# A threshold attention with two gated layers behind it: one triple of cast weights kept on chip, whole-bank ranks, and three edits behind the attention

## The chip, the cores and the metric

One core of one Trainium2 chip runs the whole program. The metric is device time in microseconds (us) of one execution, the median over runs.

## The reference, cut to what matters

```python
def _attn_ref(q, k, v, tau):                       # 4 batches, 8 heads, 576 rows, head size 64
    scores = np.matmul(q, k.transpose(0, 1, 3, 2)) / np.sqrt(q.shape[-1])
    thresh = np.max(scores, axis=-1, keepdims=True) - tau
    scores = np.where(scores >= thresh, scores, -1000000000.0)
    attn = softmax(scores)
    return np.matmul(attn, v)

x = attn_out as 2304 tokens x 512
gate = 1 / (1 + np.exp(-(x @ w_gate)))             # 512 x 1536
x = (gate * (x @ w_val)) @ w_out                   # 512 x 1536, 1536 x 512
h = ((x @ w1) * (x @ w2)) @ w3                     # 512 x 1024, 512 x 1024, 1024 x 1024
out = h @ w_out2                                   # 1024 x 512
```

The weights arrive in 64 bits, q, k and v in 32 bits.

## The kernel before, in words

Matmuls of fp32 accuracy are made from halves: `split` (line 818) rounds a block to fp32r on ScalarE (`hi`, line 822) and subtracts on GpSimd or VectorE (`lo`, line 823), and `three` (line 825) adds the three products hi x lo, lo x hi and hi x hi in one PSUM bank. All matmuls have line 439 in the profile, so they are told apart by the names of their tiles.

**The attention.** Sixteen pairs of heads with nine slices each, 144 slices. A slice is scores on TensorE (`ps_s`, from `xq`, `yq`, `xk`, `yk`, or for the ninth slice of a pair the block-diagonal `qbd`), a maximum on VectorE (line 687), two ScalarE passes (lines 695 and 696), a split into two fp16 halves on ScalarE and GpSimd (lines 703 and 707), a DMA transpose (line 711, tile `pt`) and the product with v (`u` or `ps_s`, fp16; a PV run below). Two buffers, `ps_s0` and `ps_s1`, serve all slices in turn. At the end of a pair TensorE transposes the result (`ps_x`, `ps_s` from `ident`), and ScalarE copies it to `XR` (lines 774 and 776).

**Filler beside it.** `merge_gen` first multiplies w3 by w_out2 once for all tokens (`ps<-wo,t`), and stores the merged blocks to DRAM (`sc_m`). Then `l1_gen` (line 937) computes the gated layer in four passes over tokens: three of 512 tokens, and a last one of 768 tokens that runs behind the attention. In a pass, twelve blocks F follow each other; a block is `h_unit` (24 matmuls in two banks `ps_h`), and after each third block `o_stage` (line 1077) adds three blocks' products with w_out to the tokens: four `o_unit`s with 9 matmuls each into a bank `ps_o`, and a VectorE addition into `XR`. A stage is held in `pend` and emitted after the next block's `h_unit`. So the last stage of the third pass is emitted after the first block of the last pass.

**Cast weights.** In the first pass the 64-bit weights are loaded in blocks (`XR<-in_moe_w...`, 512 KB) and cast on VectorE, ScalarE and GpSimd (`cast64`, line 796) into a triple `w` of a gate, a value and an output block (768 KB, two buffers). `usplit` (line 981) splits a block and stores the finished triple to DRAM (`sc_w`, line 989); in the later passes `uload32` (line 975) loads the triple back (line 979). `tick` (line 996) spreads these steps over the matmuls. All these DMAs are issued on SP's queue, in order, with the transposes and the loads of q, k and v.

**The order.** Up to the end of the attention the order of every engine is made by the class `Plan`: `order` (line 229) lists the instructions by a forecast of times, taking among the ready ones that of the lowest rank; `backward` (line 322) turns that into new ranks, by the latest start; `pin` (line 365) does this ROUNDS times (line 38) and pins the order with the earliest forecast end of TensorE. `kind` (line 185) names a matmul's form: H for 16 bits, T for plain fp32, R for fp32r of 64 rows, and W for other fp32r. Behind the attention the order is made by the framework's scheduler, which takes ready instructions by their place in the program.

**Behind the attention.** The last pass runs beside the preparation of w1 and w2 (`w12_gen`). Then three groups of 768 tokens follow. A group is a seven-product scheme for x @ w1 and x @ w2 (`pair`, `ps_ab`) on operands made by `x2split` (line 1331: two subtractions on VectorE, two on GpSimd, and seven splits), their product split into `abh` and `abl`, and the output stage (`ps_y`): for each of eight merged blocks `part` does 18 matmuls. `wm_load` (line 1461) loads a merged block and splits it into `wm`, which has two buffers; the split of block i + 2 is emitted behind part i. The last two parts are taken together, tile by tile, each tile going out as it is done.

Of the kernel before, what the change touches and what calls it, by code (L numbers as in the profile page):

```python
# [8 lines left out]
F32 = mybir.dt.float32  # L9
F32R = mybir.dt.float32r  # L10
F16 = mybir.dt.float16
BF16 = mybir.dt.bfloat16
I32 = mybir.dt.int32
# [8 lines left out]
class Plan:  # L22
# [12 lines left out]
    STAY = 0  # L35
    NEAR = ("HH", "RH", "TH", "HT", "RT", "TT")
    TURN = {"HW": 86, "RW": 199, "WR": 90, "HR": 90, "TR": 90, "RH": 100, "RT": 145, "TW": 5, "HT": 34}
    ROUNDS = 6

    def __init__(self, insts, cut, over, beads=()):  # L40
        self.later = [i for i in insts[cut:] if i.opcode in self.OPS]
# [280 lines left out]
    def backward(self):  # L322
        N, E = len(self.x), ("PE", "DVE", "ACT", "POOL", "SP")
        pred = [self.hard[n] | self.soft[n] for n in range(N)]
        out = [0] * N
        for n in range(N):
            for q in pred[n]:
                out[q] += 1
        lat = [d - s for s, d in zip(self.start, self.done)]
        held = [  # L330
            c[0] if e in ("PE", "SP") else max(60, c[0] - self.OVER[e])
            for c, e in zip(self.cost, self.e)
        ]
        ready, begin = [0.0] * N, [0.0] * N
        avail = {e: [n for n in range(N) if not out[n] and self.e[n] == e] for e in E}
        free = dict.fromkeys(E, 0.0)
        for _ in range(N):
            best = None
            for e in E:
                if not avail[e]:  # L340
                    continue
                n = min(avail[e], key=lambda n: (
                    max(ready[n] + lat[n] - held[n] - free[e] - 1, 0), -self.done[n]
                ))
                s = max(free[e], ready[n] + lat[n] - held[n])
                if best is None or s < best[0]:
                    best = s, e, n
            s, e, n = best
            avail[e].remove(n)
            begin[n] = free[e] = s + held[n]  # L350
            for q in pred[n]:
                out[q] -= 1
                if q not in self.hard[n]:
                    r = begin[n] - lat[q]
                elif self.e[q] == self.e[n] != "SP":
                    r = begin[n] - (lat[q] - 5 if e == "PE" else 0)
                else:
                    r = begin[n] + self.LAG[self.e[q]] + self.LEAD[e]
                ready[q] = max(ready[q], r)
                if not out[q]:  # L360
                    avail[self.e[q]].append(q)
        for i, n in enumerate(sorted(range(N), key=lambda n: -begin[n])):
            self.rank[n] = i

    def pin(self, tc):
        best = None
        for i in range(self.ROUNDS):
            seq = self.order()
            end = max(t for t, e in zip(self.done, self.e) if e == "PE")
            if best is None or end < best[0]:  # L370
                best = end, seq, self.start
            if i + 1 < self.ROUNDS:
                self.backward()
# [25 lines left out]
def kernel(  # L399
# [22 lines left out]
    nc = tc.nc  # L422
    P = 128
    B, H, S, D = q.shape
    NPAIR = H // 2
    NT, DM = out.shape
# [3 lines left out]
    NF = DFF // P  # L430
# [40 lines left out]
    ap_ = actx.enter_context(tc.tile_pool(name="attn", bufs=1, side="right"))  # L471
# [309 lines left out]
    UW = KC * P  # L781
    sc_w = [dram.tile([P, 3, UW], F32, name=f"sc_w{f}") for f in range(NF)]
# [51 lines left out]
    def flush(keep):  # L834
        while len(defer) > keep:
            defer.pop(0)()
# [84 lines left out]


    SG = 3
    lp = None
    lx = None
    lb = None
# [8 lines left out]
        lx = lx_ctx.enter_context(tc.tile_pool(name="lx", bufs=1))  # L935

    def l1_gen():
        w32, whl, gv, pend, raws = {}, {}, {}, [], {}
        NFT = B * NF
        units = []  # L940
        for F in range(NFT + 1):
# [2 lines left out]
        def unit(n):  # L944
            if n < len(units) and 0 <= units[n][1] < NFT:
                nm, F = units[n]
                return nm, F, F // NF, F % NF
            return None
# [8 lines left out]

        def packed(n):
            m = n // 3
            if m not in w32:  # L960
                w32[m] = lp.tile([P, 3, UW], I32, tag="w", name="w", bufs=2)
                w32.pop(m - 2, None)
            return w32[m]

        def ucast(n):
            u = unit(n)
# [7 lines left out]

        def uload32(n):
            m, j = divmod(n, 3)
            if unit(n) and m >= NF and j == (2 if m == NFT else 0):
                ks = slice(j, 2 if m == NF else 3)
                nc.sync.dma_start(packed(n)[:, ks].bitcast(F32), sc_w[m % NF][:, ks])

        def usplit(n):
            u = unit(n)
            if u:
                nm, F, b, f = u
                m, j = divmod(n, 3)
                x = w32[m][:, j]
                if b == 0 and j == (2 if m else 1):
                    ks = slice(2 if m == NF else 0, j + 1)
                    nc.sync.dma_start(sc_w[m % NF][:, ks], w32[m][:, ks].bitcast(F32))
                k = 4 if nm == "o" else 2  # L990
                hi = lp.tile([P, KC, P], F32R, tag=nm + "h", name=nm + "h", bufs=k)
                lo = lp.tile([P, KC, P], F32R, tag=nm + "l", name=nm + "l", bufs=k)
                split(hi, lo, x.bitcast(F32).rearrange("p (a b) -> p a b", a=KC))
                whl[nm, F] = (hi, lo)
# [7 lines left out]
        def xsplit(b):  # L1002
            o, k, w = passes[b]
            xh, xl = (lx.tile([P, KC, k * w], F32R, tag=z, name=z) for z in ("xh", "xl"))
            for j in range(k):
                js = slice(j * w, (j + 1) * w)
                for c in range(KC):
                    split(
                        xh[:, c, js], xl[:, c, js], XA[:, c, o + j * w:o + (j + 1) * w],
                        nc.vector if c % 2 else nc.gpsimd,  # L1010
                    )
            return xh, xl
# [41 lines left out]
        def o_unit(b, st_, c, j):  # L1054
            p0, k_, w = passes[b]
            ps = bank("ps_o")
            for i in range(SG):
                F = b * NF + st_ * SG + i
                hi, lo = whl["o", F]
# [33 lines left out]
        for F in range(NFT):  # L1093
            b, f = divmod(F, NF)
            if f == 0:
                while not ready(b):
                    yield None
                if b == B - 1:
                    lx_ctx.close()
                    open_lx()  # L1100
                xhl = xsplit(b)
            k, w = passes[b][1:]
            gv[F] = [
                tuple(
                    (lx if j else lb).tile([P, w], F32R, tag=g, name=g, bufs=4)
                    for g in ("gvh", "gvl")
                )
                for j in range(k)
            ]
            for j in range(k):  # L1110
                yield from h_unit(F, xhl, j)
            whl.pop(("g", F)), whl.pop(("v", F))
            if pend:
                yield from o_stage(*pend.pop())
            if f % SG == SG - 1:
                pend.append((b, f // SG))
                if F == NFT - 1:
                    flush(0)
                    yield from o_stage(*pend.pop())
                    flush(0)  # L1120
# [150 lines left out]
    NG = NT // GT  # L1271
# [86 lines left out]
    x2 = None  # L1358
    while x2 is None or l1 is not None:
        l1 = run(l1, 4200.0)  # L1360
        if next(wg_, "end") == "end" and x2 is None:
            wctx.close()
            xp = ctx.enter_context(tc.tile_pool(name="xp", bufs=1, side="right"))
            x2 = x2split(0)
# [3 lines left out]
    sp = ctx.enter_context(tc.tile_pool(name="sp", bufs=1))  # L1368
# [90 lines left out]
            at, c0, left = at + m, c0 + m, left - m  # L1459

    def wm_load(i):
        t = sp.tile([P, 2, DM], F32R, tag="wm", name="wm", bufs=2)
        x = sp.tile([P, DM], F32, tag="y", name="wms", bufs=4)
        nc.sync.dma_start(x, sc_m[i])
        split(t[:, 0], t[:, 1], x, nc.gpsimd if i % 2 else nc.vector)
        return t
# [3 lines left out]
    for g in range(NG):  # L1470
        abs_ = [
            tuple(sp.tile([P, GT], F32R, tag=f"ab{z}{f}", name=f"ab{z}{f}") for z in "hl")
            for f in range(NF2)
        ]
        for i in range(NPR):
            if i == NPR - 1:
                wms = [wm_load(0), wm_load(1)]
            pair(x2, i, abs_)
        if g + 1 < NG:
            x2 = x2split(g + 1)  # L1480
        pss = [bank("ps_y") for _ in range(GT // P)]
        def part(i, t):
            h, l = abs_[i]
            ts_ = slice(t * P, (t + 1) * P)
            three(
                pss[t], (h[:, ts_], l[:, ts_]), (wms[i][:, 0], wms[i][:, 1]), i == 0, i == NF2 - 1
            )

        for i in range(NF2 - 2):
            for t in range(GT // P):  # L1490
                part(i, t)
            wms.append(wm_load(i + 2))
        end = len(nc.cur_bb.bb.instructions)
        for t in range(GT // P):
            part(NF2 - 2, t)
            part(NF2 - 1, t)
            out_rows(g, t, pss[t])
# [36 lines left out]
```

## Time and profile before

| what | before |
|---|---|
| median of 3 runs | 1044.69 us (1042.97 to 1045.5) |
| the profiled execution | 1041.44 us |
| its span, first to last instruction | 1039.5 us |
| granted TensorE clock, mean | 0.995 of full |
| TensorE busy | 985.5 us, 95% |
| GpSimd, ScalarE, VectorE busy | 699.3, 652.9, 616.7 us |

The page gives busy times of one execution: PE is TensorE's matmuls, PEld its weight loads, DVE VectorE, ACT ScalarE, POOL GpSimd, SP the queue that issues the DMAs. Matmuls are pipelined, so that the duration of one is longer than the step to the next; the step is what counts in a full stretch. An idle time stands with what ended it.

### The profile page before, as it was taken

The page shows a single profiled execution, that of the slowest core. Times are in us where ns is not written, and L with a number is a line of the kernel's source. Part 1 is how long each engine was busy: PE and PEld are TensorE (multiplying, and loading weights), DVE is VectorE, ACT ScalarE, POOL GpSimd, SP SyncE. Part 2 cuts the span into 40 slices and gives each one's busy share as a digit, 9 for nine tenths or more (in the row PEclk, how much of TensorE's full clock was granted, in tenths as well). Part 3 has the DMA queues.
Part 4 walks back from the last instruction along what each step waited for, and adds up shares of the span by engine and source line. Part 5 has one row for each costly group of instructions (what it writes and reads, how often), then busy time and mean ns, then how long its engine had stood idle before and what let it go on. Part 6 is the DMA issues. An engine that isn't in the chain of part 4 may idle for free.

```text
span 1039.5 us, 20101 instructions
## 1 busy us (share of the span) xinstructions
PE 985.5 (95%) x7152; PEld 834.5 (80%) x7152; DVE 616.7 (59%) x1158; ACT 652.9 (63%) x1327; POOL 699.3 (67%) x595
## 2 busy tenths in 40 slices
PE   3699978999999999999999989999999999999997
PEld 2456546777777778777877889999999989989996
DVE  7877856676765444465443367767766716743741
ACT  5888978998899878799788545545422422422221
POOL 4865877999989976878887657758654804642530
PEclk9999989999999999999999999999999999999999
DMA  8999999999999986769865656665668529826922
GB/s 234 241 216 250 249 255 232 247 244 265 236 249 221 229 164 150 161 141 205 178 137 135 135 180 226 233 223 193 222 228 256 167 91 323 247 79 195 311 71 61
DMA packets 295444, 210.01 MB, mean 202 GB/s; under 512 B 220592, under 2 KB 249264, under 8 KB 295344
## 3 DMA queue, kind: packets, MB, share of 16 engines
q1 hardware_dynamic: 294944, 208.07, 77.8%
q8 instruction: 57, 0.93, 0.4%
q10 hardware_dynamic: 400, 0.66, 0.2%
q14 instruction: 43, 0.35, 0.1%
HBM read 133.17 MB, written 30.93 MB: 158 GB/s over the span
## 4 chain that ended last, share of the span: by engine, by line
PE 71%; ACT 7%; issue 6%; POOL 5%; DVE 5%; DMA 5%; SPq 1%; POOLq 0%; DVEq 0%; ACTq 0%
PE ps_h L439 25%; PE ps_ab L439 15%; PE ps_o L439 12%; PE ps_y L439 6%; PE ps_s L439 6%; PE u L439 3%; ACT ps_s L695 2%; ACT e L696 2%; DMA XR<-in_moe_w_out_dram 2%; PE ps L439 2%; POOL h L707 1%; DMA XR<-in_moe_w_dram 1%; DVE e L687 1%; DMA XR<-in_moe_w_val_dram 1%; ACT h L703 1%
## 5 line engine op out<-in xcount | busy, mean ns | idle before, releaser
L707 POOL TENSOR_TENSOR h<-e,h 128x576 f16<-128x576 f32 x144 | 184.5, 1289 | 70.8 <-ACT h L703 39.7
L687 DVE TENSOR_SCALAR_CACHE_REDUCE e<-ps_s,tauc 128x576 f32<-128x576 f32 x144 | 114.8, 813 | 77.5 <-PE ps_s L439 22.8
L695 ACT ACTIVATE ps_s<-ps_s,nt 128x576 f32<-128x576 f32 x144 | 101.7, 711 | 48.4 <-DVE e L687 47.8
L696 ACT ACTIVATE e<-ps_s,ebias 128x576 f32<-128x576 f32 x144 | 106.7, 743 | 4.0
L703 ACT ACTIVATE h<-e 128x576 f16<-128x576 f32 x144 | 97.5, 686 | 1.6 <-DMA pt<-h 1.0
L439 PE MATMUL ps_h<-xl,gh 128*128 128x512 f32 (+1 forms) x240 | 92.1, 384 | 2.5 <-POOL xl L823 2.5
L439 PE MATMUL ps_y<-wm,abh 128*128 128x512 f32 x288 | 91.7, 391 | 1.7 <-POOL wm L823 1.4
L439 PE MATMUL ps_h<-xl,vh 128*128 128x512 f32 (+1 forms) x240 | 91.5, 381 | 1.7 <-DVE yk L593 1.2
L439 PE MATMUL ps_o<-gvl,oh 128*128 128x512 f32 (+1 forms) x240 | 90.1, 376 | 1.5 <-DVE XR L1070 1.5
L439 PE MATMUL ps_o<-gvh,ol 128*128 128x512 f32 (+1 forms) x240 | 89.3, 372 | 0.0
L439 PE MATMUL ps_h<-xh,vl 128*128 128x512 f32 (+1 forms) x240 | 89.2, 372 | 0.0
L439 PE MATMUL ps_h<-xh,gl 128*128 128x512 f32 (+1 forms) x240 | 89.1, 371 | 0.0
L439 PE MATMUL ps_h<-xh,gh 128*128 128x512 f32 (+1 forms) x240 | 89.0, 371 | 0.0
L439 PE MATMUL ps_h<-xh,vh 128*128 128x512 f32 (+1 forms) x240 | 89.0, 371 | 0.0
L439 PE MATMUL ps_o<-gvh,oh 128*128 128x512 f32 (+1 forms) x240 | 88.8, 371 | 0.0
L439 PEld LDWEIGHTS <-pt 128*128 128x128 f16 x2240 | 73.5, 99 | 19.1 <-issue 17.0
L823 POOL TENSOR_TENSOR gl<-w,gh 128x512 fp32r<-128x512 f32 x42 | 54.4, 1294 | 25.8 <-ACT gh L822 25.2
L823 POOL TENSOR_TENSOR gvl<-gr,gvh 128x512 fp32r<-128x512 f32 (+1 forms) x48 | 60.2, 1255 | 13.0 <-ACT gvh L822 12.5
L822 ACT ACTIVATE abh<-r 128x384 fp32r<-128x384 f32 x48 | 24.2, 521 | 69.2 <-DVE r L1397 69.1
L439 PEld LDWEIGHTS ps_y<-wm,abh 128*128 128x128 f32 x288 | 54.1, 188 | 13.2 <-POOL wm L823 1.9
L439 PE MATMUL ps<-wo,t 128*128 128x512 f32 x128 | 62.6, 607 | 0.0
L439 PE MATMUL ps_s<-xk,xq 64*128 64x288 f32 x256 | 36.8, 362 | 26.0 <-ACT e L696 23.5
(191 smaller groups left out, 2797.7 us busy)
## 6 DMA issues: line engine op xcount, KB each, us to landing
wc<-sc_c SPq DMA_DIRECT2D x168, 256.0 KB, 3.3
w<-sc_w SPq DMA_DIRECT2D x35, 768.0 KB, 5.0
sc_c<-wc SPq DMA_DIRECT2D x56, 256.0 KB, 2.8
XR<-in_moe_w_out_dram SPq DMA_DIRECT2D x20, 512.0 KB, 5.3
sc_w<-w SPq DMA_DIRECT2D x11, 768.0 KB, 6.6
XR<-in_moe_w_dram SPq DMA_DIRECT2D x16, 512.0 KB, 5.3
raw<-in_moe_w_dram SPq DMA_DIRECT2D x16, 512.0 KB, 4.4
XR<-in_moe_w_gate_dram SPq DMA_DIRECT2D x12, 512.0 KB, 4.8
```

What stands on the lines that cost most here:

```text
L439: return nc.tensor.matmul(out_, lhsT, rhs, start=first, stop=last)
L687: nc.vector.tensor_scalar(e, x["ps"], tauc, None, op0=ALU.add, op1=ALU.min, accum_out=nt)
L695: nc.scalar.activation(x["ps"], x["ps"], AF.Prelu, scale=-1.0, bias=x["nt"], alpha=STEEP)
L696: nc.scalar.activation(x["e"], x["ps"], AF.Exp, bias=ebias, accum_out=prep[pr]["sum"][:, s:s + 1])
L703: nc.scalar.activation(x["h16"][:, 0:S], x["e"], AF.Copy)
L707: nc.gpsimd.tensor_tensor(hb[:, S:2 * S], st[g]["e"], hb[:, 0:S], op=ALU.subtract)
L822: nc.scalar.activation(hi, x, AF.Copy)
L823: (lo_eng or nc.gpsimd).tensor_tensor(lo, x, hi.bitcast(F32), op=ALU.subtract)
```

## The change

- The first block but one of each pass has its triple in a tile of its own (`k1`, in the attention's pool). It is cast there in the first pass, read from there in the first three, stored to `sc_w` in the second (for the last pass, which loads it), and not loaded in the second and third.
- In `backward`, the ranks of all W matmuls that write one PSUM tensor are set to the lowest among them, with their own rank as a tie-break. ROUNDS goes from 6 to 10.
- At the start of the last pass the pending output stage is emitted ahead of the first block.
- `wm` has three buffers, and `x2split` of the next group is emitted behind part 1 of the output stage instead of ahead of it.

```diff
-    ROUNDS = 6
+    ROUNDS = 10
...
         for i, n in enumerate(sorted(range(N), key=lambda n: -begin[n])):
             self.rank[n] = i
+        low = {}
+        for n in range(N):
+            if self.form[n] == "W":
+                t = self.io[n][1][0].tensor.name
+                low[t] = min(low.get(t, N), self.rank[n])
+        for n in range(N):
+            if self.form[n] == "W":
+                self.rank[n] = low[self.io[n][1][0].tensor.name] + self.rank[n] * 1e-6
...
+    KEEP = (1,)
...
         def packed(n):
             m = n // 3
+            if kept(m):
+                if m not in stay and m < NF:
+                    stay[m] = ap_.tile([P, 3, UW], I32, tag=f"k{m}", name="w", bufs=1)
+                return stay[m % NF]
...
+        def kept(m):
+            return m % NF in KEEP and m < (B - 1) * NF
...
-            if unit(n) and m >= NF and j == (2 if m == NFT else 0):
+            if unit(n) and m >= NF and not kept(m) and j == (2 if m == NFT else 0):
...
-                x = w32[m][:, j]
-                if b == 0 and j == (2 if m else 1):
+                x = packed(n)[:, j]
+                if b == (m % NF in KEEP) and j == (2 if m else 1):
                     ks = slice(2 if m == NF else 0, j + 1)
-                    nc.sync.dma_start(sc_w[m % NF][:, ks], w32[m][:, ks].bitcast(F32))
+                    nc.sync.dma_start(sc_w[m % NF][:, ks], packed(n)[:, ks].bitcast(F32))
...
                 xhl = xsplit(b)
+            if F == (B - 1) * NF and pend:
+                flush(0)
+                yield from o_stage(*pend.pop())
...
-        t = sp.tile([P, 2, DM], F32R, tag="wm", name="wm", bufs=2)
+        t = sp.tile([P, 2, DM], F32R, tag="wm", name="wm", bufs=3)
...
-        if g + 1 < NG:
-            x2 = x2split(g + 1)
...
             wms.append(wm_load(i + 2))
+            if i == 1 and g + 1 < NG:
+                x2 = x2split(g + 1)
```

## Rows read from the trace of the kernel before

**Rows 1.** The page: TensorE's busy time, and 40 slices of DMA in tenths.

```profile
PE 985.5 (95%) x7152; PEld 834.5 (80%) x7152; DVE 616.7 (59%) x1158; ACT 652.9 (63%) x1327; POOL 699.3 (67%) x595
...
DMA  8999999999999986769865656665668529826922
```

**Rows 2.** Busy times by stage: length, PE, PEld, DVE, ACT, POOL, PEclk, DMA share, GB/s.

```profile
130.00:165.00 35.00, 24.52 (x269) 17.49 (x266) 21.39 (x46) 28.69 (x59) 23.18 (x21) 0.85 1.08 241
165.00:312.00 147.00, 140.29 (x1245) 111.72 (x1242) 100.09 (x205) 132.64 (x268) 138.13 (x114) 1.00 1.08 249
312.00:598.00 286.00, 285.82 (x2482) 227.80 (x2478) 134.97 (x294) 232.24 (x474) 226.54 (x187) 1.00 0.78 168
598.00:620.00 22.00, 19.28 (x100) 17.44 (x100) 13.98 (x19) 11.65 (x24) 10.69 (x10) 1.00 0.50 161
620.00:1040.00 420.00, 413.34 (x2247) 395.23 (x2245) 245.27 (x377) 142.28 (x288) 214.48 (x186) 1.00 0.60 196
```

**Rows 3.** Waits from 130 to 312 us: total, times, longest.

```profile
PE ps_s L439 <- ACT e L696: 10.6, 5, 4.7
DVE ps_c L804 <- DMA XR<-in_moe_w_out_dram: 9.9, 7, 3.0
...
DVE w L810 <- DMA sc_w<-w: 3.5, 3, 2.3
```

**Rows 4.** DMA issues: count, KB each, us to landing.

```profile
w<-sc_w SPq DMA_DIRECT2D x35, 768.0 KB, 5.0
...
sc_w<-w SPq DMA_DIRECT2D x11, 768.0 KB, 6.6
```

**Rows 5.** TensorE's timeline at turns, first and last return: start, us, instruction.

```profile
312.12 0.47 PE L439 MATMUL ps_h<-xl,gh 128*128 128x512 f32 x1
312.44 0.39 PE L439 MATMUL ps_h<-xh,gl 128*128 128x512 f32 x1
...
321.94 0.39 PE L439 MATMUL ps_o<-gvh,ol 128*128 128x512 f32 x1
322.25 0.53 PE L439 MATMUL ps_s<-xk,xq 64*128 64x288 f32 x4
...
323.25 0.50 PE L439 MATMUL ps_o<-gvh,oh 128*128 128x512 f32 x1
323.58 0.40 PE L439 MATMUL ps_o<-gvl,oh 128*128 128x512 f32 x1
...
589.49 0.48 PE L439 MATMUL ps_h<-xl,gh 128*128 128x512 f32 x1
```

**Rows 6.** Timelines of GpSimd, TensorE, ScalarE, and the chain, at the seam.

```profile
597.23 1.26 POOL L823 TENSOR_TENSOR gvl<-gr,gvh 128x512 fp32r<-128x512 f32 x1
...
598.44 0.66 PE L763 MATMUL ps_x<-ident,xn 128*128 128x128 f32 x4 [0.27 <-DVE xn L748]
601.55 0.45 PE L439 MATMUL ps_h<-xl,gh 128*128 128x384 f32 x1 [2.45 <-POOL xl L823]
...
599.13 0.69 ACT L774 ACTIVATE XR<-ps_x,vi 128x512 f32<-128x512 f32 x1 [0.30 <-PE ps_x L763]
...
610.14 8.20 PE ps_o L439 x36
```

**Rows 7.** Timelines of ScalarE, TensorE and GpSimd in the last output stage.

```profile
1021.07 0.63 ACT L822 ACTIVATE wm<-wms 128x512 fp32r<-128x512 f32 x1 [3.40 <-PE ps_y L439]
...
1025.41 0.39 PE L439 MATMUL ps_y<-wm,abh 128*128 128x512 f32 x1
1027.23 0.51 PE L439 MATMUL ps_y<-wm,abh 128*128 128x512 f32 x1 [1.43 <-POOL wm L823]
...
1025.91 1.26 POOL L823 TENSOR_TENSOR wm<-wms,wm 128x512 fp32r<-128x512 f32 x1 [6.87 <-ACT wm L822]
```

**Rows 8.** TensorE and GpSimd around the second group's output stage.

```profile
919.62 0.50 PE L439 MATMUL ps_y<-wm,abh 128*128 128x512 f32 x1 [0.27 <-DVE wm L823]
...
L823 POOL TENSOR_TENSOR o3l<-x,o3h 128x768 fp32r<-128x768 f32 x1 | 2.6, 2570 | 0.0
```

More of the change, by code (lines that the diff above doesn't have):

```diff
@@ L937, in l1_gen @@
     def l1_gen():
-        w32, whl, gv, pend, raws = {}, {}, {}, [], {}
+        w32, whl, gv, pend, raws, stay = {}, {}, {}, [], {}, {}
         NFT = B * NF
```

## The prediction

> **What bounds the kernel now.** I read the page first: TensorE is busy for 95% of the span, and the DMA engines are saturated in the first third of it only [rows 1]. An average says nothing of where an edit pays, so I cut the span by stage [rows 2]: from 312 us to the end TensorE is covered but for the seam at 598 to 620 (19.28 of 22.00 us); from 130 to 165 it works 24.52 of 35.00 us at a granted clock of 0.85, partly at the lower of its two levels, and from 165 to 312 it works 140.29 of 147.00 us. The DMA share is 1.08 in both early stretches and 0.78 after. So behind 312 us time is won only by TensorE doing less (fewer turns between kinds of matmul) or by closing a hole; ahead of it, also by making something it waits for come sooner. The waits [rows 3] name what that is: TensorE waited 10.6 us for the attention's exponentials, and VectorE, which stands ahead of those in its own queue, sat idle 9.9 us for raw `w_out` blocks and 3.5 us for a store of cast weights.
>
> The sum is made against the profiled execution: its span is 1039.5 us, 1041.44 us with what lies around it. The median of the three runs shown is 1044.69 us, 3.25 us above it; I carry the difference in time over to the median. A measurement of this kernel can tell about 0.3% from no change, here 3.1 us.
>
> **The change, part by part.**
>
> *Last pass: the pending output stage goes first (tail seam).* Now TensorE ends the attention with four transposes from 598.44 us (at about 0.11 us each, so free at 598.9) and starts the pass at 601.55, after 2.45 us of waiting for the first `xl` [rows 6]. The stage put in front is 36 matmuls, 8.20 us where it now stands. Its last input, `gvl` of the last block, starts at 597.23 and takes 1.26 us, so it is there by 598.5. If the stage begins at 598.9, the hole of 601.55 - 598.9 = 2.65 us is filled and the split of `x` runs behind 8 us of matmuls. Bounds: a stage that needs a PSUM bank which the last ScalarE copy of the attention holds (to 599.13 + 0.69 = 599.8) wins 1.7 us; a stage that slips ahead of the transposes wins up to 601.55 - 597.5, less their own 0.5, so 3.5. Its four additions on VectorE sit beside the `xl` splits, covered by the same 8.20 us. I take **2.5**.
>
> *Merged weights: three buffers.* In the last group TensorE starts a matmul at 1025.41 and the next at 1027.23 instead of 0.23 us later: 1.59 us lost, because the split of the last merged block waits for the buffer of the block before the previous one [rows 7]. With a third buffer that split can begin where the one before it began, at 1021.07, 4.1 us sooner than the GpSimd half at 1025.91 needs it; the hole goes. Nothing later than the output drain follows. Bounds 1.4 and 1.7; I take **1.6**.
>
> *The split of x for the next group, moved behind two output parts.* It competes with the last products of the pair; in group 2 of 3 the output stage started about 0.4 us late (0.27 of it a wait) behind a VectorE split [rows 8]. The gain is at most that. By the code the moved work has five GpSimd operations (two subtractions and three of seven low halves), none longer than the 2.57 us of `o3l` [rows 8], so under 13 us; it now has six parts of 18 matmuls, 18 x 0.228 = 4.1 us each, 24.6 us in all, as cover. Without that cover it would cost its 13 us. Queued behind it are the splits of merged blocks 4 and 5, which the third buffer makes early by 4.1 us, more than one operation in their way. I take **0.4**, bounds -1 and 0.5.
>
> *The kept triple.* It takes one 768 KB store out of the first pass, puts it in the second in place of a load of the same size, and drops a second load in the third; SP issues one DMA fewer in each of the first and third pass (35 full loads and 11 full stores before [rows 4]). Behind 312 us no TensorE wait hangs on a load and the DMA engines have room, so these two are worth nothing there; their cover is TensorE's own work, and they can only help. In the first pass the DMA engines have none to spare: 768 KB at the 241 GB/s of the stretch [rows 2] is 3.3 us of their time, and up to the 3.5 us that VectorE waited for such stores [rows 3] may go too. Bounds: 0, because these waits are one part of a loop in which ScalarE and GpSimd are nearly as full (132.64 and 138.13 of 147.00 us [rows 2]), and 6.8. What is late next is the raw load behind it in SP's queue. I take **1.5**, near the lower end, because TensorE itself waits for little of this in the 147 us.
>
> *Ranks and ten rounds.* The planner lists TensorE's work by rank; now every matmul of a full-height fp32r bank takes its bank's lowest rank, so a bank once begun is finished unless something more urgent is ready. (The single attention slices on `qbd` count as such too, and share two tensor names through the whole kernel: they get the rank of the first ever and always go first. That costs nothing, they are urgent anyhow.) The rows show what a visit to another kind of work costs. After a PV run, the first weight matmul at 312.12 is followed only 0.32 us later, 0.09 more than 0.228. A visit to a score group stretches the matmul ahead of it to 0.31 us and the one behind it to 0.33, 0.18 in all [rows 5]. Between 312 and 598 us there are 96 such returns to weights, the first at 312.12 and the last at 589.49 [rows 5]; 37 follow or contain a score group and can't be avoided. If all others joined one of those, 59 x 0.09 = 5.3 us would go, and 16 between 165 and 312 give 1.5 more: at most 6.8. The Trainium skill ("TensorE: Matmul & The Clock Gate", Part 2) says that the queue pulls weight loads ahead of running matmuls, so that the next weights load under the present one. Taken alone, a turn would then cost nothing and this part would give 0; the longer steps beside each turn [rows 5] speak against it. On the other side stands a delay of the scores, priced as a rival below. I take **2.0**, under a third of the upper end, because banks will also end where no other work is ready. The rounds only let the planner choose from more orders by its own forecast; I give them nothing.
>
> Sum: 2.5 + 1.6 + 0.4 + 1.5 + 2.0 = 8.0 us. On the profiled execution 1033.4, on the median **1036.7 us**.
>
> **The rivals.**
> 1. *Turns and kept triple pay nothing.* Then the three edits behind the attention remain: 4.5 us, 1040.2 us. For it: both have a lower bound of 0. Against: the longer steps beside each turn [rows 5]. The chance is 0.20. By the Trainium skill's rule on weight loads ("TensorE: Matmul & The Clock Gate", Part 2) the turns' 2.0 us alone would go, 1038.7 us.
> 2. *The new plan is worse where TensorE isn't full.* From 130 to 312 us it is idle for 10.5 + 6.7 = 17.2 us; the new order shuffles DMA issues and VectorE's queue there. If it is idle a quarter longer, 4.3 us, the edits behind the attention are eaten: 1044.5 us. For it: each idle piece hangs on one late load. Against: there is as much to win. The chance is 0.18.
> 3. *Slower: banks hold the scores back.* A bank of 12 matmuls is 2.7 us; a score group that becomes ready inside one waits 1.4 on average. With 24 groups visited between 165 and 312 us that is 33 us of lateness; the exponentials' chain sets the end for perhaps a quarter of that stretch (an estimate from TensorE's 10.6 us of waits [rows 3]), 8 us. With 4.5 gained: 1048.2 us. It decides once TensorE's idle time from 130 to 312 grows past 17.2 + 4.5 us. Against: behind 312 us a late score costs nothing, as TensorE has other work [rows 2]. The chance is 0.13.
> 4. *The edits at the seam do nothing,* since the instruction order behind the attention is made by a scheduler that may have put both orders alike: 2.9 us less than forecast, 1039.6 us. The chance is 0.05; the 2.45 us wait [rows 6] is what speaks against it.
>
> **How the numbers follow.** The forecast gets the rest, 0.44, with its own range from 1030 to 1041 by the bounds. Rivals 1 and 4 are mostly faster by over 3.1 us, rival 2 is the same, rival 3 slower: faster 0.44 + 0.20 + 0.02 = 0.66, same 0.18 + 0.03 = 0.21, slower 0.13. The range from 1029 to 1046 takes in rivals 1, 2 and 4 and leaves out rival 3 and both edges.
>
> **What would show it.** Right: the first matmul behind the attention's transposes is one of `ps_o` at about 599 us of the old clock, and no `xl` wait; no hole ahead of the last merged block; the returns to weights between 312 and 598 us fall from 96 to about 75; the DMA wait of `ps_c` shrinks in the first pass; 33 full loads and 11 full stores of `sc_w`. Wrong: TensorE's idle time from 130 to 312 us grown by more than 4 us, or the number of returns unchanged.

## The result, and the profile after

The median of the changed kernel is 1030.28 us (5 runs, 1029.01 to 1032.17); the kernel before had 1044.69 (5 runs, 1040.44 to 1045.5). The ratio is 0.9874, with a 95% interval from 0.9848 to 0.9900. It is worked out from all the runs, so it is not the quotient of the two medians, which is 0.9862; it makes the gain 13.2 us (10.4 to 15.9). The same kernel in a second session gave 0.9888, from 0.9872 to 0.9904. The forecast was 1036.7 us, a gain of 8.0; the gain is 10.3 us between the two profiled executions (1041.44 to 1031.14) and 14.4 between the medians. The sign and the largest places were right, and the size was too small.

From the page of the kernel after: TensorE's and the DMA engines' rows, and the issues of cast weights (count, KB each, us to landing). They answer to [rows 1] and [rows 4].

```profile
PE 983.8 (96%) x7152; PEld 841.3 (82%) x7152; DVE 615.0 (60%) x1158; ACT 656.4 (64%) x1327; POOL 700.7 (68%) x595
...
DMA  8999999999999888678866656675668529818822
...
w<-sc_w SPq DMA_DIRECT2D x33, 768.0 KB, 5.1
...
sc_w<-w SPq DMA_DIRECT2D x11, 768.0 KB, 5.1
```

TensorE is busy 1.7 us less, and the span is 10.2 us shorter: most of what went is idle time. Two full loads are gone and no full store, as the edit says. Busy times by stage, in the columns and stretches of [rows 2]:

```profile
130.00:165.00 35.00, 25.29 (x258) 17.23 (x257) 24.19 (x51) 31.12 (x65) 27.98 (x24) 0.95 1.04 263
165.00:312.00 147.00, 142.87 (x1202) 116.40 (x1202) 98.69 (x201) 130.75 (x265) 139.24 (x114) 0.97 1.07 253
312.00:598.00 286.00, 286.00 (x2519) 232.23 (x2518) 133.83 (x296) 237.35 (x478) 223.59 (x184) 1.00 0.77 162
598.00:620.00 22.00, 22.00 (x123) 21.24 (x122) 18.64 (x25) 14.11 (x31) 14.07 (x14) 1.00 0.56 180
```

The seam at 598 to 620 is full (19.28 of 22.00 us before). Between 130 and 312 TensorE's idle time fell from 17.2 to 13.8 us. The waits of that stretch after the change, TensorE's and VectorE's (total, times, longest), which answer to [rows 3]:

```profile
PE ps_s L447 <- ACT e L704: 5.9, 5, 2.6
PE ps_h L447 <- POOL xl L831: 3.7, 2, 3.1
PE ps L447 <- DVE yk L601: 2.4, 1, 2.4
...
DVE ps_c L812 <- DMA XR<-in_moe_w_gate_dram: 2.0, 2, 1.5
DVE ps_c L812 <- DMA XR<-in_moe_w_val_dram: 1.9, 2, 1.5
```

The wait for exponentials went from 10.6 to 5.9 us, and VectorE's waits for `w_out` blocks (9.9 us) and for stores (3.5) are no longer there (in a second profile of the same kernel, e9 below, each is 1.3). Part of it came back: TensorE now waits 3.7 us for the split of x at the start of the first pass. Its timeline there:

```profile
164.75 0.50 PE L447 MATMUL ps_h<-xl,gh 128*128 128x512 f32 x1 [3.13 <-POOL xl L831]
```

From 593 us to the end the list of TensorE's waits is empty; before it held five, 4.7 us together.

The seam, TensorE's timeline after the change, which answers to [rows 6]:

```profile
593.39 0.48 PE L447 MATMUL ps_o<-gvl,oh 128*128 128x512 f32 x1
593.70 0.40 PE L447 MATMUL ps_o<-gvh,ol 128*128 128x512 f32 x1
...
595.98 0.39 PE L447 MATMUL ps_o<-gvh,oh 128*128 128x512 f32 x1
596.21 0.27 PE L775 MATMUL ps_s<-ident,xt 128*128 128x128 f32 x1
596.32 0.60 PE L771 MATMUL ps_x<-ident,xn 128*128 128x128 f32 x4
596.67 0.48 PE L447 MATMUL ps_o<-gvl,oh 128*128 128x512 f32 x1
...
602.02 0.39 PE L447 MATMUL ps_o<-gvh,oh 128*128 128x512 f32 x1
602.25 0.33 PE L447 MATMUL ps_h<-xl,gh 128*128 128x384 f32 x1
```

Twelve of the 36 matmuls of the output stage slip in ahead of the transposes, the other 24 follow them, and `ps_h` starts without a wait. The output groups, in the chain that ended last (start, length, work):

```profile
752.20 58.27 PE ps_ab L447 x336
810.46 32.65 PE ps_y L447 x144
843.11 58.24 PE ps_ab L447 x336
901.35 12.25 PE ps_y L447 x54
913.60 0.35 PE ps_ab L447 x2
913.95 20.46 PE ps_y L447 x90
934.41 57.90 PE ps_ab L447 x334
992.31 32.66 PE ps_y L447 x144
1024.96 0.02 issue
1024.99 0.69 DVE y L1464
```

It is TensorE's own work without a gap: the second group's output stage starts where the products end, and the last one's 144 matmuls run through, where the wait of [rows 7] was. So for the two profiled executions the time went at three places: the last product with v begins at 593.4 instead of 597.5 us (4.1); from there to the start of the last of the 36 `ps_o` and the first 48 `ps_h` it takes 17.1 instead of 20.5 us (3.4); from the start of the first `ps_ab` to that of the last `ps_y` 272.5 instead of 275.0 (2.5). Together 10.0 of the 10.2 us of span.

### The profile page after: what moved, and what is told of

Same layout as the page of the kernel before. It is cut to its first block, busy times and chain, and to the rows that moved or that the text cites. A ratio compares the mean times of both kernels' runs of the same rounds, so it can differ in the third digit from the quotient of the medians.

```text
span 1029.3 us, 20081 instructions
## 1 busy us (share of the span) xinstructions
PE 983.8 (96%) x7152; PEld 841.3 (82%) x7152; DVE 615.0 (60%) x1158; ACT 656.4 (64%) x1327; POOL 700.7 (68%) x595
## 4 chain that ended last, share of the span: by engine, by line
PE 79%; ACT 1%; POOL 0%; DVE 0%; issue 0%
PE ps_h L447 27%; PE ps_ab L447 17%; PE ps_o L447 15%; PE ps_y L447 10%; PE ps_s L447 6%; PE u L447 3%; PE ps_t L546 1%; PE ps_x L771 0%; ACT e L704 0%; ACT ps_s L703 0%; POOL w L821 0%; PE ps_s L556 0%; ACT xh L830 0%; POOL h L715 0%; POOL vl L648 0%
## 5 line engine op out<-in xcount | busy, mean ns | idle before, releaser
L695 DVE TENSOR_SCALAR_CACHE_REDUCE e<-ps_s,tauc 128x576 f32<-128x576 f32 x144 | 114.4, 815 | 45.9 <-PE ps_s L447 20.5
L447 PEld LDWEIGHTS <-pt 128*128 128x128 f16 x2240 | 76.5, 100 | 18.0 <-issue 14.1
L447 PE MATMUL ps_y<-wm,abh 128*128 128x512 f32 x288 | 89.4, 389 | 0.0
L1056 DVE SCALAR_TENSOR_TENSOR gr<-th,ps_h 128x512 f32<-128x512 f32 (+1 forms) x60 | 37.9, 632 | 77.0 <-PE ps_h L447 42.8
L831 POOL TENSOR_TENSOR gvl<-gr,gvh 128x512 fp32r<-128x512 f32 (+1 forms) x48 | 60.2, 1255 | 10.3 <-ACT gvh L830 9.8
L831 POOL TENSOR_TENSOR abl<-r,abh 128x384 fp32r<-128x384 f32 x24 | 24.8, 1031 | 56.0 <-ACT abh L830 54.0
```

The lines of the kernel that those rows point to most:

```text
L447: return nc.tensor.matmul(out_, lhsT, rhs, start=first, stop=last)
L695: nc.vector.tensor_scalar(e, x["ps"], tauc, None, op0=ALU.add, op1=ALU.min, accum_out=nt)
L831: (lo_eng or nc.gpsimd).tensor_tensor(lo, x, hi.bitcast(F32), op=ALU.subtract)
L1056: nc.vector.scalar_tensor_tensor(r, t, 1.0, pss["v"][:, 0:w], op0=ALU.add, op1=ALU.mult)
```

## The experiments

All are set against the kernel before in their own session, by the ratio with its 95% interval. The same places were read from every profile. "End" is the time at which the last product with v begins; "busy" and "idle" are TensorE's from 0 to that end, in which every kernel has 4805 to 4808 matmuls on record; "seam" and "groups" are the two lengths just named. A "return" is a weight matmul (into `ps_h` or `ps_o`) right behind other work of TensorE; they are counted from 165 us to the end of the attention, good to about two.

Several kernels have the same instruction order on all five queues up to the end of the attention, so their rows show how far one order moves from run to run: before and e1; after, e2, e9 and e10; e4 and e6; e5 and e12. Behind the attention there are two orders, that of before (also e2, e3, e4) and that of after (the ten others).

| kernel | ratio | end | busy | idle | seam | groups | returns |
|---|---|---|---|---|---|---|---|
| before | 1 | 597.5 | 552.5 | 45.0 | 20.5 | 275.0 | 136 |
| after | 0.9874 (0.9848 to 0.9900) | 593.4 | 552.3 | 41.1 | 17.1 | 272.5 | 102 |
| e1_behind | 0.9927 (0.9904 to 0.9951) | 602.2 | 556.7 | 45.5 | 17.1 | 272.5 | 135 |
| e2_order | 0.9976 (0.9958 to 0.9994) | 594.3 | 550.9 | 43.4 | 20.5 | 275.3 | 102 |
| e3_keep | 0.9974 (0.9958 to 0.9990) | 594.2 | 552.8 | 41.4 | 22.1 | 275.0 | 137 |
| e4_ranks | 0.9956 (0.9935 to 0.9978) | 596.6 | 553.1 | 43.5 | 22.0 | 275.0 | 101 |
| e5_no_ranks | 0.9904 (0.9887 to 0.9920) | 589.9 | 554.6 | 35.3 | 17.1 | 272.5 | 137 |
| e6_no_keep | 0.9877 (0.9857 to 0.9898) | 591.5 | 551.3 | 40.2 | 17.1 | 272.5 | 101 |
| e7_store_first | 0.9868 (0.9854 to 0.9883) | 590.4 | 553.0 | 37.4 | 17.1 | 272.5 | 98 |
| e8_keep_sixth | 0.9872 (0.9857 to 0.9887) | 590.9 | 549.7 | 41.2 | 17.1 | 272.5 | 101 |
| e9_after_again | 0.9888 (0.9872 to 0.9904) | 592.2 | 551.2 | 41.0 | 17.1 | 272.5 | 102 |
| e10_x_split_back | 0.9902 (0.9878 to 0.9925) | 593.7 | 552.9 | 40.8 | 17.1 | 272.5 | 102 |
| e11_twenty_rounds | 0.9865 (0.9845 to 0.9885) | 592.5 | 550.6 | 41.9 | 17.1 | 272.5 | 95 |
| e12_slices_out | 0.9883 (0.9863 to 0.9903) | 594.2 | 557.0 | 37.2 | 17.1 | 272.5 | 137 |

### The edits behind the attention alone: e1_behind

On the kernel before:

```diff
+            if F == (B - 1) * NF and pend:
+                flush(0)
+                yield from o_stage(*pend.pop())
...
-        t = sp.tile([P, 2, DM], F32R, tag="wm", name="wm", bufs=2)
+        t = sp.tile([P, 2, DM], F32R, tag="wm", name="wm", bufs=3)
...
-        if g + 1 < NG:
-            x2 = x2split(g + 1)
         pss = [bank("ps_y") for _ in range(GT // P)]
...
             wms.append(wm_load(i + 2))
+            if i == 1 and g + 1 < NG:
+                x2 = x2split(g + 1)
```

> The kernel before with the three edits behind the attention alone: the pending output stage first in the last pass, three buffers for the merged weights, the split of x behind two output parts. Theory (the parts add up): the traces of before and after put these at 3.6 us for the seam, 1.6 us for the last merged block and 0.9 us elsewhere in the output stages, so about 6 us faster than before, and the returns to weights stay at 96 between 312 and 598 us. Rival A (the seam's gain belongs to the new order of the attention): 2.5 us or less. Rival B (the prediction's own sizes): 4.5 us.

Measured: 1035.55 us, 0.73% of 1042.69, or 7.6 us; the interval says 5.1 to 10.0. The two lengths behind the attention give 3.4 + 2.5 = 5.9 of it. This profiled execution ended its attention 4.7 us later than that of before, with the same order of instructions: that part of the time moves from run to run (below). What follows: by the two ratios (7.6 of 13.2 us) these edits are more than half of the gain, and what the two lengths take is the same 17.1 and 272.5 us in every kernel that has them. The same edits on two other orders of the attention give about as much: 8.2 us from e4 to e6, and 7.7 to 10.6 from e2 to the changed kernel and its repeats.

### The two edits of the order: e2_order, e3_keep, e4_ranks

On the kernel before. e3_keep has the kept triple with all its lines (`KEEP`, `kept`, `packed`, the store moved to the second pass) and 6 rounds:

```diff
+    KEEP = (1,)
...
+            if kept(m):
+                if m not in stay and m < NF:
+                    stay[m] = ap_.tile([P, 3, UW], I32, tag=f"k{m}", name="w", bufs=1)
+                return stay[m % NF]
...
-                if b == 0 and j == (2 if m else 1):
+                if b == (m % NF in KEEP) and j == (2 if m else 1):
```

e4_ranks has the ranks and the ten rounds:

```diff
-    ROUNDS = 6
+    ROUNDS = 10
...
+        for n in range(N):
+            if self.form[n] == "W":
+                self.rank[n] = low[self.io[n][1][0].tensor.name] + self.rank[n] * 1e-6
```

e2_order has both.

> The kernel before with the kept triple, the ranks and ten rounds, nothing behind the attention. Theory: 3.9 us faster, TensorE's last product with v ends at 593.5 us of the span in place of 597.5, the hole of some 2.5 us at the seam is still there, as is the hole ahead of the last merged block. Rival (edits do not add up): under 1 us or over 7 us faster.

> The kernel before with the kept triple alone (six rounds, old ranks). Theory: the first pass gets shorter by what the DMA engines no longer do, 1 to 3 us in all; the returns to weights stay near 96. Rival (a new plan is a draw of the lot): anything from 5 us faster to 5 us slower, with no shorter DMA waits of VectorE.

> The kernel before with the ranks and ten rounds alone. Theory: returns to weights fall from 96 to about 75 between the start of the second pass and the end of the third, and the time by 2 to 3 us. Rival 1 (banks hold the scores back): TensorE's idle time from 130 to 312 us grows by more than 2 us and eats it, same or slower. Rival 2 (a draw of the lot): the returns fall, yet the time moves by another amount than 0.09 us for each.

Measured: the kept triple alone 0.26% (2.7 us, interval 1.0 to 4.4), the ranks alone 0.44% (4.6 us, 2.3 to 6.8), both together 0.24% (2.5 us, 0.6 to 4.4). The ten rounds alone were not timed: built without one of the two other edits, they give the order of before, instruction for instruction. With the kept triple they do count: e5_no_ranks below differs from e3_keep up to the end of the attention by the ten rounds alone, and its order is another one. So e4 is the ranks with ten rounds, and what ten rounds do to the kept triple without the ranks and without the edits behind the attention was not timed. What follows: each pays alone, and the two don't add up. That the ranks alone are better than both (0.9956 and 0.9976) is not shown; the intervals overlap.

The profiles of e3 and e4 show one thing more, at the seam that they don't change. TensorE's timeline of e3_keep there:

```profile
595.17 0.66 PE L763 MATMUL ps_x<-ident,xn 128*128 128x128 f32 x4 [0.27 <-DVE xn L748]
598.28 0.44 PE L439 MATMUL ps_h<-xl,gh 128*128 128x384 f32 x1 [2.45 <-POOL xl L823]
...
599.32 0.52 PE L439 MATMUL ps_h<-xh,gh 128*128 128x384 f32 x1
599.64 0.52 PE L439 MATMUL ps_h<-xl,vh 128*128 128x384 f32 x1
```

and TensorE's busy time, granted clock, DMA share and GB/s in two stretches behind it:

```profile
599.00:602.50 3.50, 3.50 (x13) 0.53 0.97 329
602.50:606.00 3.50, 3.50 (x21) 0.99 0.03 10
```

Behind the hole of 2.45 us the clock is granted at 0.53 for 3.5 us, which is nearly all at the lower of its two levels (1.2 GHz, not 2.4), and matmuls of 384 columns go from a step (one start to the next) of 0.17 to one of 0.32 us. So the seam costs 22.1 us there (22.0 in e4, at 0.50 from 600.60 to 604.00), where it cost 20.5 in before and e2, whose clock stayed at 1.00 behind the same hole. None of the ten profiles without a hole shows it. Closing the hole is therefore worth 3.4 us in some runs and 5.0 in others.

### One edit taken out of the changed kernel: e5_no_ranks, e6_no_keep, e10_x_split_back

On the changed kernel. e5_no_ranks, with ten rounds and the rest as they are:

```diff
-        low = {}
-        for n in range(N):
-            if self.form[n] == "W":
-                t = self.io[n][1][0].tensor.name
-                low[t] = min(low.get(t, N), self.rank[n])
-        for n in range(N):
-            if self.form[n] == "W":
-                self.rank[n] = low[self.io[n][1][0].tensor.name] + self.rank[n] * 1e-6
```

e6_no_keep takes back the lines of e3_keep's diff. e10_x_split_back:

```diff
+        if g + 1 < NG:
+            x2 = x2split(g + 1)
         pss = [bank("ps_y") for _ in range(GT // P)]
...
-            if i == 1 and g + 1 < NG:
-                x2 = x2split(g + 1)
```

> The kernel after with the old ranks (ten rounds, kept triple and the edits behind the attention stay). Theory: returns to weights back near 96, 2 to 3 us slower than after, so about 8 us faster than before. Rival (ranks do nothing but redraw the plan): within 1 us of after, or off by more than 4.

> The kernel after without the kept triple. Theory: 1 to 3 us slower than after, lost in the first pass, where VectorE waits longer for raw blocks; returns to weights as in after. Rival (the DMA relief is hidden): within 0.5 us of after.

> The kernel after with the split of x for the next group back ahead of the output stage; three buffers stay. The order of the attention is the same as in after, so only the stretch of the output groups is to be read. Theory: of the 2.5 us won there, 1.6 to 2.0 are the third buffer's and 0.5 the moved split's, so 273.0 us in place of 272.5 and no hole ahead of the last block. Rival (the third buffer alone frees the second group's start as well): 272.5.

Measured: none of the three can be told from the changed kernel. For e10_x_split_back there is a plain reason. Its trace has the order of the changed kernel, instruction for instruction, on all five queues from start to end: the framework's scheduler, which makes the order behind the attention, put the split of x at the same place from either position in the program. So this edit is none, and 0.9902 is a third measurement of the changed kernel. The chain of e10_x_split_back, in the columns above:

```profile
843.50 58.24 PE ps_ab L447 x336
901.74 12.25 PE ps_y L447 x54
913.99 0.35 PE ps_ab L447 x2
914.34 20.46 PE ps_y L447 x90
```

So the moved split is worth nothing because it moves nothing, and the third buffer has all of the 2.5 us: with it the splits of merged blocks run one part ahead. ScalarE's timeline of the changed kernel in the last output stage has them at

```profile
1008.72 0.63 ACT L830 ACTIVATE wm<-wms 128x512 fp32r<-128x512 f32 x1 [3.50 <-PE ps_y L447]
1012.75 0.63 ACT L830 ACTIVATE wm<-wms 128x512 fp32r<-128x512 f32 x1 [3.40 <-PE ps_y L447]
```

and the last of them begins 20.6 us behind the stage's first matmul (992.14). Before it began at 1025.20, 24.7 us behind the first matmul (1000.47): one part later, with its GpSimd half at 1025.91 [rows 7].

The kept triple is worth nothing on top of the rest (e6). For the ranks the sums over the whole attention tell more than the median. TensorE's busy time up to the end of the attention, granted clock, DMA share and GB/s, for the changed kernel, then for e5_no_ranks:

```profile
0.00:593.40 593.40, 552.27 (x4808) 0.99 0.91 206
```

```profile
0.00:589.90 589.90, 554.56 (x4808) 0.99 0.93 208
```

Without the ranks TensorE is busy 2.3 us more, and idle 5.8 us less: 41.1 against 35.3. The waits of e5_no_ranks from 130 to 312 us show where (total, times, longest):

```profile
PE ps_s L439 <- ACT e L696: 2.2, 2, 1.7
PE u L439 <- DMA vsh<-vh: 2.0, 1, 2.0
PE ps_h L439 <- DVE yk L593: 1.8, 2, 1.3
```

It waits 2.2 us for exponentials, where the changed kernel waits 5.9, and not at all for the split of x (3.7 us). Shorter work with the ranks and longer waits is what the prediction's third rival says, at a smaller price. But that the ranks make the waits is not shown. e3_keep has no ranks either, and an order from six rounds. Its wait for exponentials up to the end of the attention, then that of e5_no_ranks:

```profile
PE ps_s L439 <- ACT e L696: 24.5, 10, 5.0
```

```profile
PE ps_s L439 <- ACT e L696: 14.7, 6, 5.0
```

The changed kernel lies between them with 18.0 us, and e3_keep is idle for as long as it (41.4 and 41.1 us). Two orders without ranks differ here by more than either does from the one with them, so the difference can't be put down to the ranks.

### The slices left out of the ranks, which did not happen: e12_slices_out, and the changed kernel once more: e9_after_again

e9_after_again is the changed kernel without an edit. e12_slices_out, at both places of the condition:

```diff
-            if self.form[n] == "W":
+            if self.form[n] == "W" and self.free(self.io[n][0][1]) == 512:
```

> The kernel after with the whole-bank rank for 512-column matmuls alone, so that the single attention slices on qbd, which share two tensor names, keep their own rank. Theory of the prediction: those slices are urgent anyhow, so within 1 us of after. Rival (going always first hurts, as they push other work back): 2 to 4 us faster. Rival (it helps the scores): 2 to 4 us slower.

> The kernel after, unchanged, beside the three others of this group. All theories: 1.0 to 1.5% faster than before; this is the time to hold the others against. The stretch from the first product of the output groups to the last of the output stage takes 272.5 us, as in every kernel with the three edits so far.

The edit was to take the single attention slices out of the rule and leave it to the weight banks. It looked at the wrong operand: its free size is 128 for every one of these matmuls, so no bank got a common rank, and the order on all five queues is that of e5_no_ranks. What the ranks of the slices do was therefore not tried. The run still serves as a second measurement of e5's order, as e9 and e10 do for the changed kernel: without ranks 0.9904 and 0.9883, with them 0.9874, 0.9888 and 0.9902. The sums repeat too: idle 35.3 and 37.2 us without, 41.1, 41.0 and 40.8 with; waits for exponentials up to the end of the attention 14.7 and 14.5 us without, 18.0, 18.4 and 17.3 with (23.9 before).

### What the kept triple does: e7_store_first, e8_keep_sixth

On the changed kernel. e7_store_first stores the kept triple in the first pass again:

```diff
-                if b == (m % NF in KEEP) and j == (2 if m else 1):
+                if b == 0 and j == (2 if m else 1):
```

e8_keep_sixth keeps another triple:

```diff
-    KEEP = (1,)
+    KEEP = (6,)
```

> The kernel after, the kept triple stored to DRAM in the first pass again instead of in the second; loads stay away. Theory (the relief of the full DMA engines in the first pass is what the triple brings): as without the triple, 1 to 3 us slower than after. Rival 1 (the free buffer of the ring is what it brings): as after. Rival 2 (a draw of the lot): neither, and the loss isn't in the first pass.

> The kernel after with another triple kept, the seventh in place of the second. Theory: the store that goes from the first pass is one of 242 us in place of 142 us, where TensorE has more other work, so 0 to 2 us slower than after. Rival (a draw of the lot): faster or slower by more than 3 us with TensorE's waits in other places.

Measured: both as fast as the changed kernel. The waits of VectorE in e7_store_first, from 130 to 312 us:

```profile
DVE ps_c L812 <- DMA XR<-in_moe_w_gate_dram: 7.8, 2, 5.5
DVE ps_c L812 <- DMA XR<-in_moe_w_out_dram: 4.8, 3, 2.5
DVE ps_c L812 <- DMA XR<-in_moe_w_val_dram: 1.4, 2, 0.9
```

These are 14.0 us of waits for raw blocks, where the changed kernel has 3.9, and yet TensorE is not idle for longer (37.4 against 41.1 us). So in the changed kernel less DMA work in the first pass pays nothing. The kept triple as a whole pays nothing there either (e6), so e7 can't say what brought e3 its 2.7 us. In e3 VectorE's waits for raw blocks did shrink, to 4.9 us (15.8 in before, 13.7 in e1 with the same order as before), and the store was not given back on that kernel. It may also be that the order decides, which the edit changes; no run separates the two.

### More rounds: e11_twenty_rounds

```diff
-    ROUNDS = 10
+    ROUNDS = 20
```

> The kernel after with twenty rounds of the planner, so with another plan by the same rules. Theory (a plan of the same rules is worth the same): within 2 us of after, returns to weights between 95 and 105 in the first three passes. Rival (a draw of the lot): 3 us or more from after, to either side.

Measured: 0.9865, with six or seven returns fewer (95), and not to be told from the changed kernel.

No run beats the changed kernel by more than the intervals leave open. e6_no_keep is as fast with less code: the kept triple can go.

## Why the prediction was right, and where its steps were off

**The seam** (2.5 taken, bounds 1.7 to 3.5) was right in place and kind, and mis-sized: 3.4 us with the clock up, 5.0 where it fell behind the hole. The step that failed is "if the stage begins at 598.9": twelve of its matmuls begin before the transposes, the case that stood there as the upper bound. The lower clock behind the hole was in none of the rows that I had read.

**Merged weights and the split of x** (1.6 + 0.4 = 2.0) came to 2.5, all of it from the third buffer. The step "in group 2 of 3 the output stage started about 0.4 us late (0.27 of it a wait) behind a VectorE split" put that lateness down to the split of x. The split named in [rows 8] is one of `wm`, and the third buffer alone takes the lateness away. The moved split, taken at 0.4, is worth nothing: in e10 it changes no instruction's place. That is the reason of the prediction's fourth rival, and it held for this edit.

**The kept triple** (1.5, bounds 0 to 6.8) measured 2.7 us alone and nothing on top of the others. Its reason, a store less where the DMA engines are full, falls for the changed kernel with e7; for the kernel before, where the triple did pay, it stays open.

**The ranks** (2.0, bounds 0 to 6.8) measured 4.6 us alone. The price of a turn holds. It can be read from single steps: from 320 us to the end of the attention, at a granted clock of 1.00, the first weight matmul behind a PV run takes 0.314 us from its start to the next one's, and one inside a run 0.227, as medians in each of the fourteen profiles; in the seam's timeline above it is the step from 593.39 to 593.70. About 36 returns fewer (100 against 136, in the means) at 0.09 us are 3.2 us, and over the profiles TensorE's busy time up to the end of the attention is 551.7 us in the mean of the nine kernels with ranks (549.7 to 553.1) and 554.7 in the five without (552.5 to 557.0), 3.0 us apart. The two bands touch, and equal orders differ by up to 4.2 us, so the means alone are no proof. The Trainium skill ("TensorE: Matmul & The Clock Gate", Part 2) says that the next weights load under the running matmul. A turn that costs nothing, as I took it to follow, is not what the steps show: each cost 0.087 us behind a PV run.

**The sum** of these two, 3.5 us, stood for terms taken apart. They aren't such terms: 2.7 and 4.6 make 2.5. Beside the three edits behind the attention the kept triple with ten rounds brings 2.4 and 4.6 us (0.9927 less 0.9904 and 0.9883), the ranks 5.2 (less 0.9877), and both 2.6, 4.1 and 5.5 (less 0.9902, 0.9888 and 0.9874), each good to about 3 us. Why they don't add up is not shown. It would fit that both take from the same idle time (45.0 us before; 41.4, 43.5 and 43.4 with one, the other and both), but one order alone has from 40.8 to 43.4 us in four profiles, and another 40.2 and 43.5.

So the total of 8.0 was low by about 1.4 us at the seam and groups in the profiled pair, and in the order it was between 0.9 too high and 2.0 too low. That the 3.5 us came near is luck in part, since the two edits don't bring it as the prediction had shared it out. What is left of the 14.4 may go with the runs of before in that session, which lay high (its medians in the other three were 1041.19 to 1042.69), and with the clock behind the hole, 1.6 us where it falls; this is not shown.

The forecast's own range, 1030 to 1041 "by the bounds", is narrower than the bounds of its terms, which add up to 1025.4 and 1042.6; the measured 1030.28 lies at its edge.

**The rivals.** The first (turns and kept triple pay nothing: 1040.2 us) and the fourth (edits at the seam do nothing) fell with e3, e4 and e1, though the fourth's reason held for the split of x. The second (the new plan worse where TensorE isn't full) fell: idle time from 130 to 312 us went from 17.2 (16.3 in e1, the same order) to 13.8 (12.7 in e9, 11.8 in e10). The third (banks hold scores back) fell by its own point of decision, since that idle time did not grow. Its mechanism is not shown: with ranks the waits for exponentials are 3.6 us longer and the idle time 4.8 us longer than with e5's order, in the means of two profiles each, but e3's order, without ranks, waits longer than both (24.5 us).

**What it would show:** the first matmul behind the transposes is one of `ps_o`, there is no `xl` wait at the seam, no hole ahead of the last merged block, 33 loads and 11 stores. The returns from the start of the second pass on went from 96 to 74, against about 75 forecast. The DMA waits of `ps_c` went from 15.8 to 3.9 us in this pair of profiles, but e7 has 14.0 of them at the same time, and the changed kernel again has 8.9 (e9) and 0.6 (e10): the sign came as said, and it was no sign of the gain.

## What to carry to other kernels

A hole at a place where nothing else competes can be priced from its edges, and its gain stays whatever else is changed: 17.1 and 272.5 us in each of ten kernels. Two edits of a planned order need not add up (2.7 and 4.6 us alone, 2.5 together); time each alone and both, and read the idle time of the whole planned stretch from several profiles before crediting either. When an edit has a plausible reason (fewer transfers where the engines are full), test the reason alone, and on the kernel where the edit pays. And compare the executed order before crediting an edit of the program: the moved split had a price in the prediction and moved no instruction.

## What the runs showed of the hardware

The clock behind the hole, above: 2.45 us without matmuls, and in two of four profiles about 3.5 us at the lower level afterwards. The price of a turn, above: 0.087 us on the first weight matmul behind a PV run, and behind a group of 64-row score matmuls 0.11 us (0.337 against 0.227 from start to start). The third is how far equal orders lie apart. Between 130 and 200 us TensorE works in pieces, and the granted clock there differs from execution to execution. TensorE's busy time, granted clock, DMA share and GB/s in that stretch for the kernel before

```profile
130.00:200.00 70.00, 57.43 (x543) 0.93 1.07 250
```

and for e1_behind, with the same order there

```profile
130.00:200.00 70.00, 59.11 (x543) 0.90 1.08 248
```

show as many matmuls in more time at a lower clock; over the whole attention e1 ended 4.7 us later, 4.2 of it as longer busy time. Over runs of one kernel this is a spread of up to 10 us (e1: 1030.37 to 1040.21, at mean clocks of 0.996 and 0.991). One run of each can't tell two orders apart here by less than that; several runs, and sums over several profiles, narrow it.
